# Fused attention, MLP and expert layer on one core: another order in the attention step, the experts' choice behind the loop, one product for two bounds

## The chip, the core and the metric

The kernel runs on one core of a Trainium2 chip. TensorE (PE) multiplies, VectorE (DVE), ScalarE (ACT) and GpSimd (POOL) do the elementwise work, SyncE (SP) issues most of the DMAs, GpSimd the indirect ones. Each engine works through its own instructions in the order of the program and waits for the others at semaphores. The metric is the time of one execution on the device in microseconds (us).

## The reference

Three layers, one behind the other, in float32. The attention's rows keep their 32 largest scores only; the last layer sends each of 2304 tokens to one of eight experts.

```python
def _attn_ref(q, k, v):                       # 4 batches, 8 heads, 576 rows, 64 wide
    scores = np.matmul(q, k.transpose(0, 1, 3, 2)) / np.sqrt(64)
    kth = np.partition(scores, -32, axis=-1)[..., -32:-31]
    scores = np.where(scores >= kth, scores, -1e9)
    attn = np.exp(scores - scores.max(-1, keepdims=True))
    attn = attn / (attn.sum(-1, keepdims=True) + 1e-9)
    return np.matmul(attn, v)

def _moe_ref(x, w_in, w_out):                 # x [2304, 512], w_in [512, 2048]
    h = x @ w_in
    return (h * np.clip(h + 3.0, 0.0, 6.0) / 6.0) @ w_out

def _moe2_ref(x, expert_emb, tau, w1, w2):    # 8 experts, 512 -> 1024 -> 512
    logits = normalised(x) @ normalised(expert_emb).T / tau
    expert_idx = np.argmax(logits, axis=1)
    gate_w = softmax(logits)[np.arange(N), expert_idx]
    for e in range(8):
        mask = expert_idx == e
        out[mask] = gate_w[mask, None] * (np.maximum(x[mask] @ w1[e], 0.0) @ w2[e])
```

## The kernel before

**Loop.** `step` (L776) runs 76 times. The attention is cut into 72 units of 128 rows and two heads each ("t" units, and "r" units that collect the last 64 rows of each batch and score twice as much). A unit passes through five steps: in step i unit i is scored (`scores`, `take`, `pairs`), unit i-1 selects (`select`, `bounds`), i-2 is masked (`relu`, `mask`), i-3 exponentiated and scaled (`expo`, `guard`, `inverse`, `scale`), i-4 transposed and multiplied with V (`turned`, `keep`, `values`, `finish`). The order of the calls in `step` is the order of instructions on each engine; nothing rearranges it inside the loop. "A step" below is one round of it.

**Selection.** `pairs` (L373) splits a row's 576 scores on VectorE into maxima and minima, so that `select` (L386) finds the 32 largest in four rounds of MAX8 (eight at a time) with MATCH_REPLACE8 between them. Round 3 then multiplies the 32nd value by 2^100 (`zb`, L405), the bias of the `relu` (L416) that makes the mask. `bounds` (L407) makes -max/8 (`nb`, L410) on GpSimd, the bias of the exponential (L426).

**Banks.** `turned` (L446) makes nine transposes a unit, three per PSUM bank, in two banks (`bank_t`) by turns, so that the third group writes the bank of the first; `keep` (L455) copies them out on ScalarE. The routing below uses the same two banks.

**MLP beside it.** Finished rows come in pairs of 128-token groups; each pair gives eight items of the MLP queue (`push_group`, L514), one taken per step, save in eight steps (`PAUSE`, L39). An item is `s1` (24 products, L530), `gate`, `swish` (L540), `large`, `small` (`gl`, L547, on GpSimd), and one step later `s2` (12 products, L563) in two halves. The MLP's weights are read in pieces and split into high and low parts in `words` and `split_w` in the first 23 steps or so.

**Routing.** Each finished group of 128 tokens pushes four pieces on the queue `side` (`route`, L580), one taken at the end of each step: `r1` transposes, `r2` the logits and the argmax (L606 to L609), `r4` the place of each token within its expert by two small products with `tri` and `ones` (L615, L616) and a running sum `acc` on GpSimd, `r5` the place's number (L626, L627) and an indirect scatter of the token's number to the table `tbl` (L628).

**Behind the loop** the MLP's remaining items run (`whole`, two `side` pieces before each), and there the framework's scheduler sets the order by its own priorities. Once 16 groups are placed, `order` (L663) sorts the experts by load; their weights are loaded, tokens gathered from `tbl` (`tokens`, L744), and the experts run (`stage1` L906, `stage2` L922).

## Time and profile before

| | us |
|---|---|
| median of 3 runs (lowest, highest) | 1187.98 (1187.89, 1189.08) |
| the profiled execution | 1184.85 |
| its span, first to last instruction | 1183.1 |
| busy: PE, DVE, ACT, POOL | 1026.0, 838.1, 732.1, 645.7 |

The span divides into the loop (to about 770 us), the rest of the MLP (to about 892 us) and the experts. Busy times are to be read by stretch: VectorE has two thirds of its work in the loop, TensorE is busy nearly throughout. TensorE's granted clock changes between 1.2 and 2.4 GHz; a clock of 0.76 in a window means that it was at the lower level for about half of it.

### The profile page before, as it was taken

To read this page: it belongs to the slowest core of one execution; us is meant where nothing else is said; L and a number is where in the kernel's file an instruction comes from. 1 tells how busy PE (TensorE), PEld (TensorE's weight loads), DVE (VectorE), ACT (ScalarE), POOL (GpSimd) and SP (SyncE) were. 2 spreads that over 40 slices of the span, in tenths; PEclk is the share of its full clock that TensorE was granted. 3 is DMA by queue.
4 is the path that set the end of the run, shared out by engine and by line. 5 is a ranking of instruction groups with operands and counts; after the bars stand their busy time and mean duration, and the time that the engine had idled before them with its cause. 6 is when DMAs were issued, how large, how long until landed. Compare 5 with 4: busy or idle time off the path is not lost. (4 is left out here: it accounts for less than half of the span.)

```text
span 1183.1 us, 21477 instructions
## 1 busy us (share of the span) xinstructions
PE 1026.0 (87%) x7224; PEld 885.8 (75%) x7224; DVE 838.1 (71%) x2714; ACT 732.1 (62%) x1518; POOL 645.7 (55%) x846
## 2 busy tenths in 40 slices
PE   2476766699999899999899999999998898999994
PEld 1354555578888788888788878889987787888883
DVE  6999977998899998899998899611244343445440
ACT  5688768777777877777877787642334343444540
POOL 5667767686777786777786766623231433113200
PEclk9966778789999999999999998999998899999997
DMA  7335555655324445424454333346781564244540
GB/s 212 120 100 174 164 177 187 195 179 197 122 90 155 127 160 184 121 89 155 115 183 157 121 92 115 110 142 178 210 276 32 187 217 171 71 176 147 174 166 20
DMA packets 97113, 176.49 MB, mean 149 GB/s; under 512 B 21135, under 2 KB 46882, under 8 KB 96991
## 3 DMA queue, kind: packets, MB, share of 16 engines
q1 hardware_dynamic: 92351, 164.90, 43.4%
q0 software_dynamic: 4640, 10.10, 2.5%
q8 instruction: 60, 0.98, 0.3%
q14 instruction: 62, 0.51, 0.1%
HBM read 155.87 MB, written 19.71 MB: 148 GB/s over the span
## 5 line engine op out<-in xcount | busy, mean ns | idle before, releaser
L420 POOL TENSOR_TENSOR s<-s,z 128x576 f32<-128x576 f32 x144 | 186.0, 1292 | 13.0 <-ACT z L416 11.5
L530 PE MATMUL bank_h<-xh,vh 128*128 128x256 f32 x576 | 172.1, 299 | 2.7 <-ACT xh L488 1.6
L530 PE MATMUL bank_h<-xh,lo 128*128 128x256 f32 x576 | 166.7, 289 | 7.1 <-DMA lo<-lo_dram 7.1
L530 PE MATMUL bank_h<-xl,vh 128*128 128x256 f32 x576 | 166.2, 288 | 0.6 <-DVE xl L489 0.6
L399 DVE MAX8 A<-left 128x8 f32<-128x288 f32 (+1 forms) x288 | 160.0, 596 | 0.0
L453 PE MATMUL bank_t<-ident,s 128*128 128x128 f32 x648 | 110.2, 297 | 53.1 <-ACT s L440 26.1
L547 POOL TENSOR_TENSOR gl<-u,gh 128x512 fp32r<-128x512 f32 x72 | 93.2, 1294 | 79.0 <-ACT gh L544 78.0
L453 PEld LDWEIGHTS bank_t<-ident,s 128*128 128x128 f32 x648 | 76.1, 149 | 75.8 <-ACT pt L458 37.7
L368 PE MATMUL ps_sc<-kst,qh 128*128 128x288 f32 x256 | 88.8, 359 | 49.1 <-ACT s L371 24.1
L536 ACT ACTIVATE u<-bank_h,half 128x512 f32<-128x512 f32 x72 | 49.5, 687 | 118.9 <-PE bank_h L530 118.9
L563 PE MATMUL y<-wh,gh 128*128 128x512 f32 x288 | 120.0, 418 | 0.0
L530 PEld LDWEIGHTS bank_h<-xh,vh 128*128 128x128 f32 x576 | 113.3, 197 | 8.1 <-issue 3.1
L530 PEld LDWEIGHTS bank_h<-xh,lo 128*128 128x128 f32 x576 | 113.2, 196 | 8.3 <-DMA lo<-lo_dram 8.3
L563 PE MATMUL y<-lo,gh 128*128 128x512 f32 x288 | 115.9, 403 | 0.0
L530 PEld LDWEIGHTS bank_h<-xl,vh 128*128 128x128 f32 x576 | 113.4, 197 | 1.4 <-DVE xl L489 1.0
L735 DVE TENSOR_TENSOR l<-a,h 128x1024 fp32r<-128x1024 f32 x64 | 77.4, 1232 | 51.9 <-ACT h L734 45.7
L563 PE MATMUL y<-wh,gl 128*128 128x512 f32 x288 | 114.2, 401 | 0.0
L416 ACT ACTIVATE z<-s,zb 128x576 bf16<-128x576 f32 x144 | 112.7, 782 | 1.0 <-DVE zb L405 0.8
L426 ACT ACTIVATE s<-s,nb 128x576 f32<-128x576 f32 x144 | 111.7, 775 | 0.0
L458 ACT COPY pt<-bank_t 128x384 f32<-128x384 f32 x216 | 95.6, 479 | 24.4 <-PE bank_t L453 24.4
L540 DVE SCALAR_TENSOR_TENSOR u<-u,bank_h 128x512 f32<-128x512 f32 x72 | 49.2, 684 | 83.8 <-ACT u L536 83.7
L471 PE MATMUL bank_a<-pt,vt 128*64 128x128 f32 (+1 forms) x1600 | 105.4, 285 | 0.0
(230 smaller groups left out, 2819.9 us busy)
## 6 DMA issues: line engine op xcount, KB each, us to landing
lo<-lo_dram SPq DMA_DIRECT2D x144, 512.0 KB, 4.3
a<-in_moe_w_dram SPq DMA_DIRECT2D x64, 512.0 KB, 8.7
kraw<-in_k_dram SPq DMA_DIRECT2D x64, 144.0 KB, 2.6
qraw<-in_q_dram SPq DMA_DIRECT2D x64, 128.0 KB, 3.3
w<-in_moe_w_in_dram SPq DMA_DIRECT2D x32, 256.0 KB, 3.9
w<-in_moe_w_out_dram SPq DMA_DIRECT2D x32, 256.0 KB, 3.5
lo_dram<-wf SPq DMA_DIRECT2D x32, 256.0 KB, 2.1
vt<-in_v_dram SPq DMA_DIRECT2D x16, 320.0 KB, 4.1
```

Source lines behind the costliest of these rows:

```text
L368: nc.tensor.matmul(ps[:, n, :HS], t, kk[:, HS * g:HS * g + HS], start=(o == 0), stop=(o == len(parts) - 1))
L399: nc.vector.max(A[:, n, 8 * r:8 * r + 8], src[:, n, :w])
L416: nc.scalar.activation(zb_[n], tile_of(i, n), AF.Relu, bias=sel[i][2][:, n:n + 1], scale=-BIG)
L420: nc.gpsimd.tensor_tensor(s, s, zb_[n], op=ALU.subtract)
L426: nc.scalar.activation(s, s, AF.Exp, bias=sel[i][1][:, n:n + 1], scale=SCALE, accum_out=sums[i][:, n:n + 1])
L453: nc.tensor.transpose(pp[:, 128 * k:128 * k + 128], e[:, 128 * (3 * c + k):128 * (3 * c + k) + 128], ident)
L458: nc.scalar.copy(pts[i][:, 3 * c:3 * c + 3, :].rearrange("p k n -> p (k n)"), tb_.pop((i, c))[:, :384])
L471: nc.tensor.matmul(av[64 * n:64 * n + 64, c0:c1], vt[:, k, 64 * n:64 * n + 64], pt[:, k + 5 * n if k < 4 else 4, c0:c1], start=(o == 0), s ...
L530: nc.tensor.matmul(ph[:, a, :], w, x[:, k, :], start=(k == 0 and n == 0), stop=(k == 3 and n == 2))
L547: nc.gpsimd.tensor_tensor(state[q][1], state.pop((q, "u")).rearrange("p (a n) -> p a n", a=2), state[q][0].bitcast(F32), op=ALU.subtract)
L563: nc.tensor.matmul(state["y"][o], x[:, a, c], w, start=(f == 0 and n == 0), stop=(f == 15 and n == 2))
L735: nc.vector.tensor_tensor(lo, x, hi.bitcast(F32), op=ALU.subtract)
```

## The change

1. **Another order of `step`.** `mask` of head 0 moves behind `select` round 0; rounds 0 and 1 no longer stand together; `relu`, `expo`, `select` and `take` are interleaved with the three `turned`/`keep` pairs, and a half of `s2` (`after`) now stands between the first and the second use of the banks, the other half behind the third. `inverse` (the reciprocal of the sums) stands before `select` round 3 instead of behind it. The `side` piece (`aside`) is taken in mid-step.
2. **One product for both bounds.** `bounds` makes `-max/8` and `2^100 * 32nd` in one GpSimd product of two operands (128x4); the two `zb` products on VectorE go. It stands behind `scale`, ahead of `mask` of head 1, and the first `relu` of the next step now waits for it.
3. **The experts' choice in batches.** `r2` ends with the copy of the logits; `r4` and `r5` go. `choose` does the argmax, the places and the scatters for all groups scored since the last call, behind the loop, for 12, 2, 2 and 2 groups. The scatters are declared independent of each other.

```diff
@@ -400,20 +406,17 @@
         if r < TOPK // 8 - 1:
             for n in range(2):
                 nc.vector.match_replace(dst[:, n, :w], A[:, n, 8 * r:8 * r + 8], src[:, n, :w], NEG)
-        else:
-            for n in range(2):
-                nc.vector.tensor_scalar(zb[:, n:n + 1], A[:, n, TOPK - 1:TOPK], BIG, None, op0=ALU.mult)
 
     def bounds(i):
 
-        A, nb, zb = sel[i]
-        nc.gpsimd.tensor_scalar(nb, A[:, :, 0], -SCALE, None, op0=ALU.mult)
+        A, nb = sel[i]
+        nc.gpsimd.tensor_tensor(nb, A[:, :, 0:TOPK:TOPK - 1], kb, op=ALU.mult)
         if not exact:
             nc.gpsimd.tensor_tensor(viol[:, i, :, :], A[:, :, TOPK - 1:TOPK].broadcast_to([128, 2, 2]), A[:, :, 15:24:8], op=ALU.subtract)
 
     def relu(i, n):
 
-        nc.scalar.activation(zb_[n], tile_of(i, n), AF.Relu, bias=sel[i][2][:, n:n + 1], scale=-BIG)
+        nc.scalar.activation(zb_[n], tile_of(i, n), AF.Relu, bias=sel[i][1][:, n, 1:2], scale=-BIG)
 
     def mask(i, n):
         s = tile_of(i, n)
...
@@ -423,7 +426,7 @@
         if n == 0:
             sums[i] = sm.tile([128, 2], F32, tag="sums", name="sums")
         s = tile_of(i, n)
-        nc.scalar.activation(s, s, AF.Exp, bias=sel[i][1][:, n:n + 1], scale=SCALE, accum_out=sums[i][:, n:n + 1])
+        nc.scalar.activation(s, s, AF.Exp, bias=sel[i][1][:, n, 0:1], scale=SCALE, accum_out=sums[i][:, n:n + 1])
 
     def guard(i):
         sel.pop(i)
...
@@ -599,39 +602,47 @@
...
             nc.vector.tensor_copy(l_all[:, g, :], p2)
-            ix = sm.tile([128, 8], U32, tag="ix", name="ix")
-            ixf = sm.tile([128, 1], F32, tag="ixf", name="ixf")
-            oh = sm.tile([128, E], BF16, tag="oh", name="oh")
-            mx = sm.tile([128, 8], F32, tag="mx", name="mx")
-            nc.vector.max(mx, l_all[:, g, :])
-            nc.vector.max_index(ix, mx, l_all[:, g, :])
-            nc.vector.tensor_copy(ixf, ix[:, 0:1])
-            nc.vector.tensor_scalar(oh, iota8, ixf, None, op0=ALU.is_equal)
-            state["oh"] = oh
-
-        def r4():
-            oh = state["oh"]
-            pq = bank()[:, :E]
-            nc.tensor.matmul(pq, tri, oh, start=True, stop=False)
-            nc.tensor.matmul(pq, ones, acc, start=False, stop=True)
-            nc.gpsimd.tensor_tensor(acc, acc, oh, op=ALU.add)
-            po = sm.tile([128, E], F32, tag="po", name="po")
-            nc.vector.tensor_tensor(po, pq, ebase, op=ALU.add)
-            state["po"] = po
-
-        def r5():
-            oh, po = state["oh"], state["po"]
-            de = sm.tile([128, 1], F32, tag="de", name="de")
-            di = sm.tile([128, 1], I32, tag="di", name="di")
-            nc.vector.scalar_tensor_tensor(po, po, 1.0, oh, op0=ALU.mult, op1=ALU.mult, accum_out=de)
-            nc.vector.tensor_copy(di, de)
-            nc.gpsimd.indirect_dma_start(out=tbl, out_offset=bass.IndirectOffsetOnAxis(ap=di[:, 0:1], axis=0),
-                                         in_=ids[:, g, :], in_offset=None)
-            done_groups[0] += 1
-            if done_groups[0] == NG - 2:
-                order()
-
-        side.extend((r1, r2, r4, r5))
+            scored[0] += 1
+
+        side.extend((r1, r2))
+
+    def choose():
+
+        g0, g1 = done_groups[0], scored[0]
+        n = g1 - g0
+        lg = l_all[:, g0:g1, :]
+
+        def wide(x):
+            return x.unsqueeze(2).broadcast_to([128, n, E])
+
+        def deep(x):
+            return x.unsqueeze(1).broadcast_to([128, n, E])
+        nc.vector.tensor_reduce(mxs[:, g0:g1], lg, axis=AX.X, op=ALU.max)
+        eq = fs.tile([128, NG, E], F32, tag="df", name="eqs")[:, :n, :]
+        nc.vector.tensor_tensor(eq, lg, wide(mxs[:, g0:g1]), op=ALU.is_equal)
+        nc.vector.tensor_tensor(eq, eq, deep(rev8), op=ALU.mult)
+        first = fs.tile([128, NG], F32, tag="gt", name="first")[:, :n]
+        nc.vector.tensor_reduce(first, eq, axis=AX.X, op=ALU.max)
+        nc.vector.tensor_tensor(picks[:, g0:g1, :], eq, wide(first), op=ALU.is_equal)
+        for g in range(g0, g1):
+            nc.gpsimd.tensor_tensor(before[:, g + 1, :], before[:, g, :], picks[:, g, :], op=ALU.add)
+        pq = half_a()[:, :n * E]
+        nc.tensor.matmul(pq, tri, picks[:, g0:g1, :].rearrange("p g e -> p (g e)"), start=True, stop=False)
+        nc.tensor.matmul(pq, ones, before[:, g0:g1, :].rearrange("p g e -> p (g e)"), start=False, stop=True)
+        po = fs.tile([128, NG, E], F32, tag="df", name="pos")[:, :n, :]
+        nc.vector.tensor_tensor(po, pq.rearrange("p (g e) -> p g e", e=E), deep(ebase), op=ALU.add)
+        nc.vector.tensor_tensor(po, po, picks[:, g0:g1, :], op=ALU.mult)
+        de = fs.tile([128, NG], F32, tag="nrm", name="de")[:, :n]
+        nc.vector.tensor_reduce(de, po, axis=AX.X, op=ALU.add)
+        nc.vector.tensor_copy(rows[:, g0:g1], de)
+        for g in range(g0, g1):
+            w_ = nc.gpsimd.indirect_dma_start(out=tbl, out_offset=bass.IndirectOffsetOnAxis(ap=rows[:, g:g + 1], axis=0),
+                                              in_=ids[:, g, :], in_offset=None)
+            tc.declare_no_dep(w_.ins, group="places", reason="every token has one place")
+            tc.add_to_no_dep_group("places", w_.ins)
+        done_groups[0] = g1
+        if g1 == NG - 2:
+            order()
 
     def whole(item, last):
 
...
@@ -785,44 +796,50 @@
                 convert_w()
 
         a = moe.popleft() if moe and i not in PAUSE else None
+        def aside():
+            if side:
+                side.popleft()()
+
+        def after(o):
+            if last:
+                last[6](last[0], o)
+
         at_(2, relu, 0)
-        at_(2, mask, 0)
         at_(3, expo, 0)
-        lows()
         split_w()
         load_k(i + 2)
         at_(1, select, 0)
-        at_(1, select, 1)
         part(a, 1)
         part(a, 2)
+        at_(2, mask, 0)
+        lows()
+        at_(4, turned, 0)
+        at_(4, keep, 0)
         part(a, 3)
         words()
-        for c in range(2):
-            at_(4, turned, c)
-            at_(4, keep, c)
+        aside()
+        part(a, 4)
+        after(0)
+        at_(4, turned, 1)
+        at_(4, keep, 1)
         at_(0, scores, 0)
         at_(4, turned, 2)
+        at_(3, expo, 1)
+        at_(1, select, 1)
+        at_(0, take, 0)
         at_(4, keep, 2)
-        at_(0, take, 0)
+        after(1)
         at_(1, select, 2)
+        part(a, 5)
+        at_(3, guard)
         words()
-        at_(3, expo, 1)
-        at_(3, guard)
-        if last:
-            last[6](last[0], 0)
-        part(a, 4)
-        part(a, 5)
         at_(0, scores, 1)
         at_(0, take, 1)
-        at_(1, select, 3)
         at_(3, inverse)
         if i - 3 >= EARLY:
             at_(3, scale)
+        at_(1, select, 3)
         at_(2, relu, 1)
-        at_(2, mask, 1)
-        at_(1, bounds)
-        if last:
-            last[6](last[0], 1)
         split_w()
         at_(0, pairs)
         words()
...
@@ -835,9 +852,9 @@
             at_(3, scale)
         at_(4, values)
         at_(4, finish)
+        at_(1, bounds)
+        at_(2, mask, 1)
         need_v(i)
-        if side:
-            side.popleft()()
         if i in (12, 14, 15, 17):
             embed((12, 14, 15, 17).index(i))
         if i == 20:
...
@@ -876,6 +895,9 @@
                 if side:
                     with tc.high_priority(offset=SIDE):
                         side.popleft()()
+                if done_groups[0] < scored[0] and scored[0] % 2 == 0:
+                    with tc.high_priority(offset=SIDE):
+                        choose()
             last = whole(moe.popleft() if moe else None, last)
             if rest and len(moe) <= 1:
                 rest = False
```

`kb` is a constant tile with -1/8 and 2^100, `rev8` one with 8 to 1, `before` holds the running sums in place of `acc`.

**VectorE, one step in mid-loop**, from the last operation of the value products (`xl`) to the next `pairs` (MAX and MATCH_REPLACE are the rounds of `select`, L540/L543 is `swish`, `sums` the reciprocal). Before:

```order
L489 TENSOR_TENSOR xl<-bank_a,xh 128x128
L399 MAX A<-top 128x8 x2
L402 MATCH_REPLACE top<-A,top 128x144 x2
L399 MAX A<-top 128x8 x2
L402 MATCH_REPLACE left<-A,top 128x144 x2
L540 SCALAR_TENSOR_TENSOR u<-u,bank_h 128x512
L399 MAX A<-left 128x8 x2
L402 MATCH_REPLACE left<-A,left 128x288 x2
L399 MAX A<-left 128x8 x2
L405 TENSOR_SCALAR zb<-A 128x1 x2
L433 RECIPROCAL sums<-sums 128x2
L380 TENSOR_TENSOR ps_sc<-ps_sc,s_144 128x2x144
```

Now:

```order
L492 TENSOR_TENSOR xl<-bank_a,xh 128x128
L405 MAX A<-top 128x8 x2
L408 MATCH_REPLACE top<-A,top 128x144 x2
L543 SCALAR_TENSOR_TENSOR u<-u,bank_h 128x512
L405 MAX A<-top 128x8 x2
L408 MATCH_REPLACE left<-A,top 128x144 x2
L405 MAX A<-left 128x8 x2
L408 MATCH_REPLACE left<-A,left 128x288 x2
L436 RECIPROCAL sums<-sums 128x2
L405 MAX A<-left 128x8 x2
L386 TENSOR_TENSOR ps_sc<-ps_sc,s_149 128x2x144
```

The two `zb` rows are gone, `swish` stands behind round 0 instead of round 1, and the reciprocal ahead of the last MAX.

**TensorE, the same place in a step**: `bank_t` are the transposes, `ps_sc` the scores, `y` the second MLP product. Before:

```order
L453 MATMUL bank_t_120<-ident,s_145 128x128 x3
L453 MATMUL bank_t_121<-ident,s_145 128x128 x3
L368 MATMUL ps_sc<-kst,qh 128x288
L368 MATMUL ps_sc<-kst,ql 128x288
L368 MATMUL ps_sc<-kst,qh 128x288
L368 MATMUL ps_sc<-kst,ql 128x288
L453 MATMUL bank_t_120<-ident,s_145 128x128 x3
L563 MATMUL y<-wh,gh 128x512
L563 MATMUL y<-lo_6130,gh 128x512
```

Now:

```order
L566 MATMUL y<-wh,gh 128x512
L566 MATMUL y<-lo_5897,gh 128x512
L566 MATMUL y<-wh,gl 128x512
L566 MATMUL y<-wh,gh 128x512
L566 MATMUL y<-lo_5897,gh 128x512
L566 MATMUL y<-wh,gl 128x512
L456 MATMUL bank_t_125<-ident,s_150 128x128 x3
L374 MATMUL ps_sc<-kst,qh 128x288
L374 MATMUL ps_sc<-kst,ql 128x288
L374 MATMUL ps_sc<-kst,qh 128x288
L374 MATMUL ps_sc<-kst,ql 128x288
L456 MATMUL bank_t_126<-ident,s_150 128x128 x3
```

Six products of `s2` stand between the first three transposes (the row ahead of these) and the second three; the scores, and the third three, follow.

**GpSimd behind the loop**: `tbl` are the scatters, `gl` the low part that `s2` waits for. Before:

```order
L547 TENSOR_TENSOR gl<-u,gh 128x512
L442 TENSOR_SCALAR s_146<-s_146,sums 128x576 x2
L547 TENSOR_TENSOR gl<-u,gh 128x512 x2
L617 TENSOR_TENSOR acc<-acc,oh 128x8
L628 DMA tbl<-ids,di 22528x2
L547 TENSOR_TENSOR gl<-u,gh 128x512
L617 TENSOR_TENSOR acc<-acc,oh 128x8
L628 DMA tbl<-ids,di 22528x2
L547 TENSOR_TENSOR gl<-u,gh 128x512 x8
```

Now:

```order
L550 TENSOR_TENSOR gl<-u,gh 128x512
L433 TENSOR_SCALAR sums<-sums 128x2
L445 TENSOR_SCALAR s_151<-s_151,sums 128x576 x2
L550 TENSOR_TENSOR gl<-u,gh 128x512
L639 DMA tbl<-ids,rows 22528x2 x12
L550 TENSOR_TENSOR gl<-u,gh 128x512 x2
L628 TENSOR_TENSOR before<-before,picks 128x8 x2
L550 TENSOR_TENSOR gl<-u,gh 128x512 x2
L639 DMA tbl<-ids,rows 22528x2 x2
L550 TENSOR_TENSOR gl<-u,gh 128x512 x7
```

Where a scatter stood alone between two `gl`, twelve now stand in a row ahead of one.

## Rows read from the trace of the kernel before

**Rows 1.** Windows of the whole run: us; busy us (count) per engine; PE clock; DMA share; GB/s
```profile
15.00:135.00 120.00, 70.91 (x365) 54.89 (x365) 117.26 (x409) 89.91 (x196) 81.75 (x107) 0.76 0.47 147
135.00:270.00 135.00, 97.91 (x686) 83.09 (x687) 116.76 (x379) 97.73 (x214) 97.74 (x129) 0.82 0.57 184
270.00:740.00 470.00, 450.11 (x3653) 390.77 (x3653) 433.55 (x1568) 360.18 (x795) 337.41 (x468) 0.99 0.42 134
740.00:900.00 160.00, 154.77 (x1097) 138.40 (x1094) 49.70 (x160) 65.88 (x128) 53.58 (x61) 1.00 0.56 175
```

**Rows 2.** Windows again: one plain step (first row), then stretches of thinner or fuller steps
```profile
335.00:344.40 9.40, 9.40 (x78) 8.17 (x77) 8.42 (x32) 6.98 (x16) 6.73 (x11) 1.00 0.38 129
353.70:371.70 18.00, 16.02 (x151) 13.76 (x150) 15.93 (x60) 13.37 (x32) 11.31 (x16) 1.00 0.57 183
390.50:431.80 41.30, 35.48 (x291) 30.46 (x290) 39.81 (x135) 32.91 (x78) 32.40 (x44) 0.96 0.47 148
528.50:546.60 18.10, 16.12 (x151) 13.80 (x150) 15.96 (x60) 13.45 (x32) 11.36 (x16) 1.00 0.57 185
565.30:605.50 40.20, 34.06 (x293) 29.04 (x292) 39.55 (x134) 32.93 (x78) 31.65 (x43) 1.00 0.50 155
694.50:708.90 14.40, 11.77 (x111) 8.85 (x110) 14.30 (x56) 12.68 (x30) 11.83 (x17) 1.00 0.28 88
```

**Rows 3.** Lines of VectorE by form: operations the change removes; busy us, mean ns
```profile
L405 DVE TENSOR_SCALAR zb<-A 128x1 f32<-128x1 f32 x144 | 19.4, 144 | 0.0
...
L626 DVE SCALAR_TENSOR_TENSOR po<-po,oh 128x8 f32<-128x8 f32 x18 | 11.4, 631 | 0.2
...
L609 DVE TENSOR_SCALAR oh<-iota,ixf 128x8 bf16<-128x8 f32 x18 | 9.3, 519 | 0.6
...
L606 DVE MAX8 mx<-l_all 128x8 f32<-128x8 f32 x18 | 3.1, 170 | 0.6
...
L607 DVE FIND_INDEX8 ix<-mx,l_all 128x8 uint32<-128x8 f32 x18 | 2.9, 160 | 0.0
L619 DVE TENSOR_TENSOR po<-bank_t,ebase 128x8 f32<-128x8 f32 x18 | 2.8, 157 | 5.6 <-PE bank_t L616 5.6
L608 DVE CAST ixf<-ix 128x1 f32<-128x1 uint32 x18 | 2.8, 153 | 0.6
L627 DVE CAST di<-de 128x1 int32<-128x1 f32 x18 | 2.7, 153 | 0.5
```

**Rows 4.** One line of VectorE, all its instructions: ns min/median/max
```profile
L626 DVE SCALAR_TENSOR_TENSOR po<-po,oh x18: 157/647/1147, 307.0 to 909.7; 128x8 f32<-128x8 f32 x18
```

**Rows 5.** Lines of GpSimd by form: the present product and the two-operand one beside it
```profile
L410 POOL TENSOR_SCALAR nb<-A 128x2 f32<-128x2 f32 x72 | 17.3, 240 | 0.0
...
L412 POOL TENSOR_TENSOR viol<-A 128x4 bf16<-128x4 f32 x72 | 15.7, 219 | 2.6 <-DVE zb L405 2.4
```

**Rows 6.** Timeline of TensorE in the plain step: start, us; third transposes of the step
```profile
340.30 0.29 PE L368 MATMUL ps_sc<-kst,ql 128*128 128x288 f32 x1
340.56 0.55 PE L453 MATMUL bank_t<-ident,s 128*128 128x128 f32 x3
```

**Rows 7.** Timelines of VectorE, ScalarE and GpSimd, same step: what the reciprocal's place decides
```profile
342.35 1.41 DVE L399 MAX8 A<-left 128x8 f32<-128x576 f32 x2
...
342.05 0.79 ACT L426 ACTIVATE s<-s,nb 128x576 f32<-128x576 f32 x1
...
343.02 0.22 POOL L430 TENSOR_SCALAR sums<-sums 128x2 f32<-128x2 f32 x1 [2.33 <-ACT s L426]
```

**Rows 8.** Timeline of GpSimd behind the loop: rhythm of gl, two indirect transfers in a row
```profile
818.49 1.29 POOL L547 TENSOR_TENSOR gl<-u,gh 128x512 fp32r<-128x512 f32 x1 [4.33 <-ACT gh L544]
...
869.90 0.99 POOL L750 DMA_INDIRECT xg<-y_dram,idt  x1 [2.03 <-DMA idt<-tbl]
871.19 0.96 POOL L750 DMA_INDIRECT xg<-y_dram,idt  x1 [0.30 <-issue]
```

**Rows 9.** Timeline of TensorE, last group's routing: its wait ahead of the product with tri
```profile
909.14 0.17 PE L615 MATMUL bank_t<-oh,tri 128*128 128x8 bf16 x1 [4.37 <-DVE oh L609]
```

More of the change, by code (lines that the diff above doesn't have):

```diff
@@ L509, in layers @@
     step = [0]
-    done_groups = [0]
+    done_groups, scored = [0], [0]
     pushed = [0]
@@ L665, in order @@
         pc = half_a()
-        nc.tensor.matmul(pc[:, :E], ones, acc, start=True, stop=True)
+        nc.tensor.matmul(pc[:, :E], ones, before[:, NG - 2, :], start=True, stop=True)
         cnt = fs.tile([1, E], F32, tag="cnt", name="cnt")
@@ L687, in finish_counts @@
         pc = half_a()
-        nc.tensor.matmul(pc[:, :E], ones, acc, start=True, stop=True)
+        nc.tensor.matmul(pc[:, :E], ones, before[:, NG, :], start=True, stop=True)
         cnt = fs.tile([1, E], F32, tag="cnt2", name="cnt2")
```

18 lines of the change are left out of this document (12 added, 6 removed).

## The prediction

> **What bounds the kernel now.** I read the windows of the whole run first, to see which engine fills which stretch, then the same view for single steps, then VectorE's lines for the price of what goes, and timelines for the places where the order changes.
>
> The windows [rows 1] show three regimes. From 15 to 135 us VectorE is busy 117.26 of 120 us: this stretch is its own. From 135 to 270 us it is busy 116.76 of 135, TensorE's granted clock is 0.82 (part of the time at 1.2 GHz), and waits for weight pieces lie between. From 270 to 740 us TensorE is busy 450.11 of 470 and VectorE 433.55, so the mean does not say which one decides. From 740 to 900 us TensorE has 154.77 of 160, VectorE and GpSimd a third each.
>
> The 470 us come apart in the single steps [rows 2]. The plain step, with a whole MLP item, has TensorE busy 9.40 of 9.40 us and VectorE 8.42: TensorE's. The five stretches below it hold the steps whose MLP item was paused and those that load new keys. There VectorE is busy 15.93 + 39.81 + 15.96 + 39.55 + 14.30 = 125.6 of 132 us, TensorE 113.5: VectorE's. In what is left of the 470 us, 338 us, TensorE is busy 450.1 - 113.5 = 336.7. So VectorE's time is worth something in 132 us of the main loop and next to nothing in the other 338.
>
> **The change, part by part.**
>
> *The two zb products* cost 19.4 us in 144 instructions [rows 3], 0.27 us a step. In the first stretch of VectorE, about 12 steps, that is 12 x 0.27 = 3.2 us. In the second, about 10 steps at a busy share of 116.76/135, it is 10 x 0.27 x 0.87 = 2.3 us. In the five stretches, 14 steps, it is 3.8 us. In the plain steps it is nothing: the cover is TensorE's 9.40 us, and VectorE would merely wait longer for the MLP's rows.
>
> *The argmax and the places* leave the loop: the other seven rows of the group add up to 35.0 us for 18 groups, 1.94 a group [rows 3]; the logits' copy stays. Twelve groups are routed between 270 and 740 us, 23.3 us; in proportion to time, 132/470 of it, 6.5 us, lies in steps that VectorE bounds. Of this 11.4 us is one operation on 8 columns whose single instructions took from 157 to 1147 ns [rows 4], so most of it was waiting. The Trainium skill has a rule for this (SBUF — State Buffer, "SBUF: two separate sides"): VectorE and GpSimd share a pair of ports under an exclusive lock, and an operation with two SBUF inputs waits while GpSimd holds it. By that rule the wait would pass to the next such operation, the whole group would be worth no more than seven times the unblocked 157 ns, 1.1 us instead of 1.94, and the sum would lose 2.8 us. I keep the 6.5, because the selection's MAX and MATCH rows, which follow in the loop, have one input.
>
> So VectorE's stretches of the main loop give 3.8 + 6.5 = 10.3 us. From below nothing excludes 0, if another engine's chain is just behind; from above TensorE's 113.5 of 132 us allow 18.
>
> *What is put in their place.* `choose` runs where VectorE is busy 49.70 of 160 us [rows 1]; its nine operations on up to 96 columns, four times, are covered there, and I cost them at nothing (without that cover 36 operations at about 0.16 us, 6 us). The product for both bounds replaces one GpSimd instruction of 240 ns by one of a kind that takes 219 ns beside it [rows 5]: nothing.
>
> *The banks.* In the plain step the third three transposes start 0.26 us after the last score product, which took its place in the pipeline in about 0.13 us [rows 6]: the rest, 0.13 us, is the wait for the copy that frees the first bank. With six products of `s2` between the two uses this wait goes; but TensorE then changes its kind of work once more per step, and the same rows show such a change costing about as much. Bounds over some 35 plain steps: 0 and -4.5 us. I take -1.5.
>
> *The new waits.* The first `relu` of a step waits for GpSimd's product where it waited for VectorE's. ScalarE is busy 6.98 of 9.40 us in a plain step [rows 2], which covers a fraction of a microsecond; queued behind that `relu` are the exponential and the MLP's `gate`, and VectorE's `swish` waits for these. The reciprocal, now ahead of the last MAX, makes VectorE wait for `guard`; see the rivals.
>
> *Scatters.* Eighteen in the loop and behind it become 12 + 2 + 2 + 2. They did not wait for each other before, being a step or more apart, so the declared independence gives nothing by itself. Two indirect transfers in a row start 1.29 us apart [rows 8], so twelve hold GpSimd for 15.5 us. Behind the loop it makes one `gl` per MLP item, 1.29 us, and idles 4.33 between [rows 8]. One `gl` is then late by 15.5 - 4.3 = 11.2 us, and `s2` waits for it. The scheduler has drawn the first MLP products of the next three items ahead of that `s2`; at half of the 5.62 us of an item each, that is 8.4 us of work. What stays is 2.8 us of idle TensorE; bounds 0 and 11.2.
>
> *The end.* The last group's product with `tri` waits 4.37 us on TensorE before [rows 9]. Now 50 products of the expert layer stand between its logits and `tri`, and 24 fewer ahead of the logits. At 5.62/36 = 0.16 us each, the 26 more are 4.1 us, which fills the wait; the chain to the gathered tokens is as long as it was, plus one scatter of 1.29 us, because both of the last pair's stand behind it. I take +1.3, between 0 and 5.
>
> **Sum.** -3.2 - 2.3 - 10.3 - 1.5 + 2.8 + 1.3 = -13.2 us. Against the profiled execution's 1184.85 that is 1171.7; the median of the runs is 3.1 higher, so 1174.8, rounded to 1175.
>
> **Rivals.**
>
> *The reciprocal becomes VectorE's new wait (slower).* In the plain step the last MAX starts at 342.35, the exponential that `guard` needs at 342.05, and `guard` itself at 343.02 and for 0.22 [rows 7]. A reciprocal asked for at 342.35 would have waited 0.9 us. For it: the slack is negative by the old timing. Against it: on ScalarE the `take` of the first half and the third copy stood ahead of that exponential and now stand behind, which brings it forward by about as much. The price at 0.9 us in the 12 + 10 + 14 steps that VectorE bounds is 32 us: 1207. It decides from 0.4 us a step on, where it eats the 13.2 and 2.4 more. Chance 0.10.
>
> *The saving is hidden.* If in the five stretches and at the start ScalarE's or GpSimd's chain stands close behind VectorE (in 390.5 to 431.8 us they are busy 32.91 and 32.40 of 41.30 [rows 2]), the 15.8 us shrink to some 5, and the 4.1 added behind the loop cancel them: 1187. For it speaks that each step is one long chain through four engines, against it that VectorE's share is 95%. Chance 0.12.
>
> *The scatters are not covered.* If the reordered MLP products run out or wait for their one bank, the whole 11.2 us fall on TensorE, and the wait at the end grows by 5: +8.4 + 3.7, 1187. Chance 0.07, counted half to no change and half to slower.
>
> *TensorE's clock comes up earlier.* In 135 to 270 us it was at the lower level for about 2 x 0.18 of the time, 49 us [rows 1]. The main loop, where TensorE is busy 450.11 of 470 us, shows 0.99. If work between the banks' uses closes some, the stretch shrinks towards VectorE's 116.76 - 2.7 = 114 us: at most 21 us, at two thirds 14. That gives 1161. The Trainium skill says the same of the cause (TensorE: Matmul & The Clock Gate, "What's actually happening"): the throttled clock is the default, and activity releases it. Against it: VectorE and the weight pieces set the pace there, and they change little. Chance 0.13.
>
> That the change does not do what it says I give no chance: the order of the instructions shows each part.
>
> **Numbers.** Forecast 0.58, at 1175; with the two unknown costs and the cover at their ends it spans 1160 to 1185. A measurement of this kernel can tell about 0.2%, 2.4 us, from no change. Faster: 0.58 + 0.13 = 0.71. Same: 0.12 + 0.04 = 0.16. Slower: 0.10 + 0.03 = 0.13. The range takes in the clock's case and the hidden one up to a little more: 1154 to 1192; outside are most of the reciprocal's case and the deep end of the clock's.
>
> **What would show it.** Right: the plain step still at 9.3 to 9.4 us with TensorE busy throughout; the five stretches shorter by a half to one microsecond a step; the stretch from 15 us on shorter by 0.27 us a step; one idle stretch of TensorE of some 3 us right behind the loop, while GpSimd issues twelve scatters. Wrong: a line of waits of the reciprocal on `guard` of more than 15 us in total; waits of `relu` on the new product; plain steps that change by more than 0.3 us either way; a granted clock in 135 to 270 us that differs by more than 0.05.

## The result: 1.0% slower on the record, and no gain in any series

| | before | changed |
|---|---|---|
| median of 4 runs, us | 1188.49 (1187.89 to 1189.08) | 1200.16 (1196.88 to 1205.69) |
| ratio, 95% interval | | 1.0103 [1.0059, 1.0147] |
| profiled execution, its span, us | 1184.85, 1183.1 | 1196.88, 1195.1 |
| forecast, us | | 1175, range 1154 to 1192 |

The changed kernel was run twice more, beside the kernel before each time (after_again, after_third below): 1.0099 [1.0067, 1.0131] and 1.0017 [0.9994, 1.0041]. In the first two of its three profiles TensorE's signals behind the loop came late; the third, which has none, is the one to read behind the loop (last section). None of the three shows the 1.1% that were forecast as a gain.

First the windows of the changed kernel, the columns as in [rows 1]:

```profile
15.00:135.00 120.00, 70.39 (x365) 55.41 (x365) 117.44 (x380) 90.05 (x195) 80.82 (x107) 0.74 0.47 147
135.00:270.00 135.00, 97.06 (x687) 81.92 (x686) 117.73 (x360) 98.55 (x214) 103.69 (x131) 0.82 0.57 186
270.00:740.00 470.00, 442.43 (x3618) 392.80 (x3617) 404.42 (x1369) 359.24 (x791) 320.99 (x444) 0.99 0.42 134
740.00:900.00 160.00, 145.38 (x1004) 129.86 (x1003) 53.21 (x137) 62.62 (x117) 65.47 (x83) 0.97 0.56 172
```

From 15 to 135 us VectorE runs 29 instructions fewer than before and is busy as long (117.44 against 117.26). From 270 to 740 us it is busy 29.1 us less, but the steps have not become shorter (next table): TensorE is busy 7.7 us less, too. The clock in the second stretch is the same 0.82. From 740 to 900 us TensorE is busy 9.4 us less.

The starts of two products, `values` (a step's last work on TensorE) and `s2` (an MLP item's), mark the stages; steps, units and items are counted from 0, and step i holds the `values` of unit i-4. Differences to the profile of before, us; the first row holds the starts in before:

| | `values` of step 10 | step 20 | step 75, the loop's last | `s2` of item 60 | end |
|---|---|---|---|---|---|
| before | 111.1 | 256.2 | 786.3 | 821.6 | 1183.1 |
| changed, on record | +0.1 | -1.3 | +0.3 | +9.3 | +12.0 |
| changed, third profile | +0.2 | +0.3 | +4.6 | +6.8 | +3.9 |
| forecast | -3.2 | -5.5 | -17.3 | -14.5 | -13.2 |

The loop misses its forecast by 17.6 us on record and by 21.9 in the third profile. Behind the loop 4.1 us more were forecast; on record it is 11.7, in the third profile 0.7 less than before. So the first question is where the 17 us went that the loop was to lose; late signals (last section) stand in the stretch of the other.

### The profile page after: what moved, and what is told of

Its sections match the earlier page's. It is cut to its first block, busy times and chain, and to the rows that moved or that the text cites. A ratio compares the mean times of both kernels' runs of the same rounds, so it can differ in the third digit from the quotient of the medians.

```text
span 1195.1 us, 21149 instructions
## 1 busy us (share of the span) xinstructions
PE 1022.0 (86%) x7196; PEld 891.6 (75%) x7196; DVE 815.8 (68%) x2443; ACT 735.5 (62%) x1518; POOL 646.3 (54%) x849
## 5 line engine op out<-in xcount | busy, mean ns | idle before, releaser
L423 POOL TENSOR_TENSOR s<-s,z 128x576 f32<-128x576 f32 x144 | 183.5, 1291 | 32.1 <-ACT z L419 30.5
L374 PE MATMUL ps_sc<-kst,qh 128*128 128x288 f32 x256 | 93.5, 376 | 69.5 <-ACT s L377 40.0
L456 PE MATMUL bank_t<-ident,s 128*128 128x128 f32 x648 | 114.7, 292 | 41.4 <-ACT s L443 27.6
L456 PEld LDWEIGHTS bank_t<-ident,s 128*128 128x128 f32 x648 | 83.2, 149 | 59.0 <-ACT s L443 33.1
L543 DVE SCALAR_TENSOR_TENSOR u<-u,bank_h 128x512 f32<-128x512 f32 x72 | 49.5, 688 | 113.8 <-ACT u L539 108.4
L377 ACT COPY s<-ps_sc 128x576 f32<-128x576 f32 x144 | 91.6, 636 | 54.0 <-PE ps_sc L374 53.0
L566 PE MATMUL y<-wh,gh 128*128 128x512 f32 x288 | 123.8, 431 | 0.0
L374 PEld LDWEIGHTS ps_sc<-kst,qh 128*128 128x128 f32 x256 | 55.8, 218 | 89.9 <-ACT s L377 42.2
L419 ACT ACTIVATE z<-s,nb 128x576 bf16<-128x576 f32 x144 | 112.1, 779 | 8.1 <-POOL nb L413 7.8
```

The costliest lines, as they stand in the source:

```text
L374: nc.tensor.matmul(ps[:, n, :HS], t, kk[:, HS * g:HS * g + HS], start=(o == 0), stop=(o == len(parts) - 1))
L377: nc.scalar.copy(sbuf[i % NS][:, :, HS * g:HS * g + HS], ps_[i][:, :, :HS])
L419: nc.scalar.activation(zb_[n], tile_of(i, n), AF.Relu, bias=sel[i][1][:, n, 1:2], scale=-BIG)
L423: nc.gpsimd.tensor_tensor(s, s, zb_[n], op=ALU.subtract)
L456: nc.tensor.transpose(pp[:, 128 * k:128 * k + 128], e[:, 128 * (3 * c + k):128 * (3 * c + k) + 128], ident)
L543: nc.vector.scalar_tensor_tensor(u, u, 1.0, state.pop((q, "h")), op0=ALU.min, op1=ALU.mult)
```

## The experiments

Theory: VectorE's saving is real, but each step is one chain through four engines, and the new order puts other work of GpSimd beside VectorE's. Rivals: one part of the change costs by itself (the choice, the bounds, the reciprocal's wait), or the scatters do.

**The three parts, each alone, on the kernel before.** The product for both bounds alone (e1):

```diff
-        nc.gpsimd.tensor_scalar(nb, A[:, :, 0], -SCALE, None, op0=ALU.mult)
+        nc.gpsimd.tensor_tensor(nb, A[:, :, 0:TOPK:TOPK - 1], kb, op=ALU.mult)
...
-        nc.scalar.activation(zb_[n], tile_of(i, n), AF.Relu, bias=sel[i][2][:, n:n + 1], scale=-BIG)
+        nc.scalar.activation(zb_[n], tile_of(i, n), AF.Relu, bias=sel[i][1][:, n, 1:2], scale=-BIG)
```

> The kernel before, with the one GpSimd product for both bounds in place of the two zb products, and nothing else. Theory 'the saving turns into port waits': VectorE loses 19.4 us of instructions, but its operations with two SBUF inputs (the kst and wf subtractions, the selection of the place) get longer, as they did in the changed kernel (kst 767 to 1006 ns, wf 502 to 583 ns); about 3 us are left: 1185 us. Rival 'the saving is real, the order eats it': 5.5 us at the start and 3.8 in the paused steps come through, 1179 us, and kst and wf keep their means within 5%. Rival 'hidden': 1188 us with VectorE idle longer.

Measured: 1210.43, 1.0176 [1.0125, 1.0228], outside all three; the loop ends 26.8 us later than before, while `kst` and `wf` keep their means (793 and 511 ns). Waits of ScalarE, 135 to 740 us (waiter <- awaited: us in total, times, longest), in this kernel:

```profile
ACT z L414 <- POOL nb L408: 67.2, 43, 4.4
```

and in the changed kernel:

```profile
ACT z L419 <- POOL nb L413: 3.3, 7, 1.7
```

In the old order `nb` stands on GpSimd behind `mask 1`, and `relu` waits for it 43 times. The new order moves `bounds` ahead of that mask; without it the part costs 1.8%.

The choice alone (e2):

```diff
-        side.extend((r1, r2, r4, r5))
+            scored[0] += 1
+        side.extend((r1, r2))
+    def choose():
```

> The kernel before, with the choice of experts batched behind the loop (12, 2, 2, 2 groups) and nothing else. Theory 'the batch stalls TensorE behind the loop': the loop ends some 5 us earlier (786 to about 781), and the twelve scatters in a row then delay one gl by 11 us, so that everything from the product with that gl on is 6 us later than before, and the end is 1194 to 1198 us. Rival 'the new order is what costs': the stall behind the loop is under 4 us here, and the time is 1180 to 1184 us.

Measured: 1187.75, 1.0006 [0.9979, 1.0033], between the two. VectorE is busy 413.00 us from 270 to 740 us instead of 433.55, and the loop ends 1.8 us earlier (3.5 and 4.5 in the profiles of e10 and e16, whose loop is the same). Most of the rest has become waits. VectorE's waits from 135 to 740 us, before:

```profile
DVE u L540 <- ACT u L536: 30.1, 26, 5.5
DVE ps_sc L380 <- ACT s L371: 6.1, 11, 1.0
...
DVE sums L433 <- POOL sums L430: 2.6, 3, 1.1
```

and with the choice taken out:

```profile
DVE u L545 <- ACT u L541: 51.9, 37, 5.0
```

`swish` waits 21.8 us more for ScalarE's `gate`: about what was saved. `gate` itself waits for TensorE's `s1`, from 270 to 740 us here

```profile
ACT u L541 <- PE bank_h L535: 67.1, 40, 4.9
```

and 66.9 us before. Only 4.8 of the 21.8 us lie in the five stretches that the prediction gave to VectorE; most of the others lie in steps where it expected this wait. Behind the loop the batch costs 9.6 us up to `s2` of item 57 and 6.7 up to item 60.

The order alone (all the moves in `step` that the diff shows, with the two `zb` products and the choice left where they were; e3):

```diff
         at_(2, relu, 0)
-        at_(2, mask, 0)
         at_(3, expo, 0)
-        lows()
...
         part(a, 2)
+        at_(2, mask, 0)
+        lows()
+        at_(4, turned, 0)
+        at_(4, keep, 0)
```

> The kernel before, with the new order of the step and nothing else (two zb products, choice in the loop). Theory 'the new order adds waits': with the second round of the selection behind swish, VectorE waits for ScalarE's gate some 18 us more, 9 us more for take and 10 us more for guard than before; plain steps are 0.2 us shorter, steps in which xl or a key is late are 1 us longer; together 1190 to 1196 us. Rival 'the order is a gain': plain steps 0.2 us shorter and nothing else, 1181 us (35 x 0.2 us).

Measured: 1198.20, 1.0087 [1.0058, 1.0116]; the loop ends 16.4 us later. The reciprocal's wait came as said (14.8 us instead of 2.6), that for `gate` by half (38.9 instead of 30.1), that for `take` did not. Then order and bounds without the choice, which stays in the loop (e4):

```diff
-        side.extend((r1, r2))
+        side.extend((r1, r2, r4, r5))
```

> The changed kernel with the choice of experts put back into the loop, one group at a time (the bounds' product and the new order stay). Theory 'the batch stalls TensorE behind the loop': without twelve scatters in a row the 11 us behind the loop are gone, the routing's 27 us of VectorE are back in the loop and cost some 5 to 8 of them: 1190 to 1196 us. Rival 'the batch is free': 1200 us or more, because the routing is back and nothing is won behind the loop.

Measured: 1193.36, 1.0057 [1.0037, 1.0077], as its theory had it; the loop +12.6 us. The parts don't add: +26.8, -1.8 and +16.4 alone, +0.3 to +4.6 together (+3.3 in the second profile). In the new order the choice does cost about 8 to 12 us in the loop, in the old one 1.8 to 4.5.

What the order does on VectorE is seen in its lines by form, 15 to 740 us (busy us, mean ns), first before, then the changed kernel:

```profile
L221 DVE SCALAR_TENSOR_TENSOR wf<-w 128x256 int32<-128x256 int32 x62 | 29.0, 502 | 4.1 <-DMA w<-in_moe_w_in_dram 3.4 <-DMA w<-in_moe_w_out_dram 0.7
...
L352 DVE TENSOR_TENSOR kst<-kraw,kst 64x288 fp32r<-64x288 f32 x28 | 20.4, 767 | 0.4
```

```profile
L227 DVE SCALAR_TENSOR_TENSOR wf<-w 128x256 int32<-128x256 int32 x62 | 33.9, 583 | 1.5 <-DMA w<-in_moe_w_out_dram 1.2 <-DMA w<-in_moe_w_in_dram 0.2
L358 DVE TENSOR_TENSOR kst<-kraw,kst 64x288 fp32r<-64x288 f32 x28 | 27.1, 1006 | 0.4
```

The same two operations, the same in form and number, take 11.6 us more: over half of the 18.9 us of `zb` in this window. (`kst`, the keys' remainder, is a part of `lows` and was moved with it.) The order alone has them at 551 and 939 ns, the choice alone at 512 and 737. And the operation on 8 columns of [rows 4] does get shorter in the new order, while another one gets longer. Before:

```profile
L626 DVE SCALAR_TENSOR_TENSOR po<-po,oh 128x8 f32<-128x8 f32 x11 | 10.2, 927 | 0.0
L609 DVE TENSOR_SCALAR oh<-iota,ixf 128x8 bf16<-128x8 f32 x11 | 7.3, 665 | 0.4
```

and with the order alone:

```profile
L609 DVE TENSOR_SCALAR oh<-iota,ixf 128x8 bf16<-128x8 f32 x11 | 14.3, 1303 | 0.4
L626 DVE SCALAR_TENSOR_TENSOR po<-po,oh 128x8 f32<-128x8 f32 x10 | 2.5, 251 | 0.0
```

The sum, 17.5 and 16.8 us, stays nearly the same, as if a wait had only changed its place.

**Single moves of the order taken back, in the changed kernel.** The forecasts of this part start from the record's 1200 us, which holds the late signals of the last section; the profiles of e5, e6, e7 and e9 have none. So the loop's end is compared, and not the time: 786.6, 789.6 and 790.9 us in the three profiles of the changed kernel. Its VectorE waits, 135 to 740 us:

```profile
DVE u L543 <- ACT u L539: 48.5, 41, 6.6
DVE ps_sc L386 <- ACT s L377: 13.3, 22, 1.5
DVE sums L436 <- POOL sums L433: 12.4, 20, 1.5
```

The second selection back beside the first (e5):

```diff
         at_(1, select, 0)
+        at_(1, select, 1)
...
-        at_(1, select, 1)
```

> The changed kernel (1200 us) with the selection's second round back beside the first, ahead of s1. Theory 'VectorE idles for gate': the second round, 1.1 us of VectorE work, again covers its wait for ScalarE's gate; the wait of swish, 48.5 us between 135 and 740 us, falls to some 30, the loop (786.6 us) gets 5 to 8 us shorter, the time is 1192 to 1195 us. Rival 'that wait is only slack of steps that TensorE bounds': the loop stays within 2 us, 1199 to 1201 us.

The reciprocal back behind the last selection (e6):

```diff
+        at_(1, select, 3)
         at_(3, inverse)
         if i - 3 >= EARLY:
             at_(3, scale)
-        at_(1, select, 3)
```

> The changed kernel with reciprocal and scale back behind the last MAX. Theory 'the reciprocal waits for guard on VectorE': its 12.4 us of waits between 135 and 740 us go, those in steps that VectorE bounds count: 3 to 6 us less, 1194 to 1197 us. Rival 'the early reciprocal helps': scale and the first transposes come 1.4 us later per step and the time grows by 3 us or more, to 1203 us.

Mask 0 and the low parts back at the head of the step (e7):

```diff
         at_(2, relu, 0)
+        at_(2, mask, 0)
         at_(3, expo, 0)
+        lows()
...
-        at_(2, mask, 0)
-        lows()
```

> The changed kernel with GpSimd's first mask of a step and the lows (the remainders of keys and queries) back ahead of the selection. Theory 'the moved mask lies beside the keys' remainder on VectorE and holds it up': kst falls from 1006 to some 770 ns and wf from 583 to 510 ns, 11 us of VectorE, of which 3 to 6 come through in the steps that load keys: 1194 to 1197 us. Rival 'the waits only change their place': another operation with two SBUF inputs gets longer by as much, 1199 to 1201 us.

Measured: 1191.82, 1.0048 [1.0023, 1.0073]; 1195.04, 1.0075 [1.0056, 1.0094]; 1183.82, 0.9980 [0.9957, 1.0003]. The loop ends 7.7 and 8.0 us later than before, and 1.2 us earlier. The first two theories fall, though the times are at the numbers forecast or next to them: the loop got longer than the changed kernel's. In e5 the wait moves from `u` to the reciprocal,

```profile
DVE sums L436 <- POOL sums L433: 53.8, 46, 3.6
DVE u L543 <- ACT u L539: 15.4, 12, 6.0
```

and in e6 from VectorE to GpSimd, whose scaling now waits for the later reciprocal (19.5 us in the changed kernel):

```profile
POOL s L445 <- DVE sums L436: 67.8, 50, 2.4
```

In e5 there is one thing more: `wf` takes 490 ns in the first stretch (15 to 135 us) instead of 608, and step 10 comes 3.1 us earlier than before, which is what the prediction gave that stretch. No other kernel has that; it is one profile.

The third theory holds for `kst`, which takes 638 ns there, less than before the change, and not for `wf` (570 ns; 619 in the first stretch). The kernels with this repair end the loop at 785.1, 783.7 and 782.2 us (e7, e11, e14). The low parts alone moved back (e12):

```diff
         at_(3, expo, 0)
+        lows()
...
-        lows()
```

> The changed kernel with the lows alone back ahead of the selection; the first mask stays where the change put it. Theory 'the key remainders, not the mask, are what was moved to the wrong place': as e7, 0.2% under before or better, kst near 640 ns on VectorE. Rival 'the mask': as the changed kernel, kst near 1000 ns.

1185.69, 0.9989 [0.9971, 1.0007]; `kst` 851 ns, between the two, so both moves lengthen it. From e12 to e7 only GpSimd's mask stands elsewhere, and `kst` on VectorE takes 213 ns less. The loop's end, +1.9 us, lies within those of the changed kernel.

The routing piece at the step's end, where it was, on order and bounds with the choice in the loop (e8, made from e4):

```diff
         words()
-        aside()
...
         need_v(i)
+        aside()
```

> The changed kernel with the choice in the loop (1193 us), and the routing pieces back at the end of the step. Theory 'pieces in the middle of the step are what made the choice dear under the new order': the loop's end falls from 12.6 us behind the kernel before to under 4 us behind, 1183 to 1187 us. Rival 'it is the rest of the order': it stays within 3 us, 1190 to 1195 us.

1198.41, 1.0078 [1.0048, 1.0109], later than both forecasts and with late signals; the loop +11.4 us against +12.6 without the move: the piece's place is not the cause.

**The twelve scatters.** In the third profile of the changed kernel GpSimd, right behind the loop:

```profile
795.90 1.22 POOL L639 DMA_INDIRECT tbl<-ids,rows  x1 [7.12 <-DVE rows L637]
797.43 0.97 POOL L639 DMA_INDIRECT tbl<-ids,rows  x1 [0.30 <-issue]
...
810.08 0.96 POOL L639 DMA_INDIRECT tbl<-ids,rows  x1 [0.30 <-issue]
811.06 2.53 POOL L550 TENSOR_TENSOR gl<-u,gh 128x512 fp32r<-128x512 f32 x2
```

Twelve in 15.2 us (15.5 by [rows 8]), and two `gl` wait for the last. They were then pulled apart, one pair behind each of the next six MLP items; each pair's rows are formed with 0 times that item's rounded hidden values added, which ties them to it (e9):

```diff
-        nc.vector.tensor_copy(rows[:, g0:g1], de)
-        for g in range(g0, g1):
+        spots.extend(range(g0, g1, 2))
...
             last = whole(moe.popleft() if moe else None, last)
+            if spots and last:
+                scatter(recent[0])
```

> The changed kernel with the twelve scatters of the first batch made to follow one another in pairs, each pair behind the gl of another MLP item (its rows are formed from the item's gh, times zero, by two small VectorE operations a pair); the choice itself stays batched. Theory 'the twelve scatters in a row stall TensorE behind the loop': the 6.0 us of idle TensorE at 804 us go, everything from there on is 6 to 11 us earlier, 1189 to 1194 us. Rival 'the items behind the loop wait for their own chain': the idle stretch stays above 4 us and the time is 1198 to 1201 us.

1190.18, 1.0029 [1.0001, 1.0058]: the time came true, but beside the changed kernel without late signals (1.0017) it is no gain. From the loop's end to `s2` of item 57 this kernel loses nothing (+2.5 to +1.7 us), the third profile of the changed one 5.1 (+4.6 to +9.7). The same in the old order with the choice batched (the edits of e2 and e9; e10):

> The kernel before with the batched choice alone (1188 us), and its first twelve scatters in pairs behind the gl of six items. Theory 'the scatters in a row are what the batch costs': the 9 us by which it fell behind at the item after the loop go, 1179 to 1183 us. Rival 'they come back in the items that now carry scatters': 1186 to 1189 us.

1191.79, 1.0008 [0.9988, 1.0027], with late signals, and the same kernel in another series (e16):

> The kernel of e10 (old order of the step, batched choice, spread scatters) in another series. Theory 'the new order with the bounds' product is worth little even when repaired': 1180 to 1184 us, within 3 us of e14's 1181. Rival 'the repaired order carries the gain': 1186 us or more, as before.

1185.95, 0.9987 [0.9967, 1.0008], at the rival's edge. From the loop's end to item 60 these two lose 0.9 and 0.4 us, where e2 lost 6.7. But it comes back: from item 60 to the end the third profile of the changed kernel and e2 gain 2.9 and 2.8 us on before, e9 and e16, with the scatters apart, lose 3.6 and 3.0 (e14 and e15 below 1.0 and 0.3). So the stall is real and the repair removes it there; that it shortens the whole is not shown.

**Together, and the kernel again.** The edits of e7 and e9 in the changed kernel, in two series (e11, e14), and the changed kernel in each (after_again, after_third). The late signals named there are shown in the last section:

> The changed kernel itself, beside the variants on the same chip. Its first profile has idle stretches of ScalarE and VectorE behind the loop that nothing in the profile ends (8.0 us before a gate, 5.0 before a swish, 27.4 before the expert layer's remainders); three variants whose code is the same there lack them and run that part 9 to 13 us faster. Theory 'they belong to that execution, not to the change': 1187 to 1193 us here. Rival 'they belong to this program': 1197 to 1203 us again, with the same stretches at the same places.

> The changed kernel with both repairs: first mask and lows early, and the scatters spread. Theory 'the two costs lie in different places and add': 1184 us less the 6 us that e7 still lost between the items at the loop's end, 1177 to 1180 us. Rival 'the spread scatters only delay later items, as the 4 us did that the first spread kernel lost at 838 us': 1183 to 1187 us.

> The changed kernel once more. Both profiles of it so far, and all four of the last series (one chip), have 14 to 19 products of TensorE behind the loop whose signal the waiting engines see 1 to 9 us late; the eight profiles of the two other series have none. Theory 'that is the chip or the execution, and half of what the changed kernel lost is not its own': beside a series without late signals it is slower than before by 0.2 to 0.6% only, 1189 to 1194 us against 1186.5. Rival 'the changed kernel brings it about, or the loss is elsewhere': slower by 0.9 to 1.2% again, 1197 to 1201 us against 1186.5.

> The kernel of e11 (early mask and lows, scatters spread) in another series. Theory 'its two repairs add where the tail is undisturbed': 1177 to 1181 us against 1186.5, 3 us or more under e12. Rival 'the spread scatters only move the wait': within 2 us of e12.

Changed: 1202.16, 1.0099 [1.0067, 1.0131], and 1189.34, 1.0017 [0.9994, 1.0041]. With both edits: 1187.88, 0.9979 [0.9949, 1.001], and 1181.07, 0.9956 [0.9936, 0.9977], without late signals. after_again came out by its rival, after_third and e14 by their theories, e11 by neither. The lines of the two conversions in e14:

```profile
L228 DVE SCALAR_TENSOR_TENSOR wf<-w 128x256 int32<-128x256 int32 x62 | 32.9, 567 | 2.8 <-DMA w<-in_moe_w_out_dram 1.4 <-DMA w<-in_moe_w_in_dram 1.4
...
L359 DVE TENSOR_TENSOR kst<-kraw,kst 64x288 fp32r<-64x288 f32 x28 | 17.3, 655 | 0.4
```

One stall of the new order was left. In the changed kernel TensorE stands still inside `s1` when two new groups begin:

```profile
346.04 0.28 PE L533 MATMUL bank_h<-xh,vh 128*128 128x256 f32 x1
347.02 0.39 PE L533 MATMUL bank_h<-xl,vh 128*128 128x256 f32 x1 [0.70 <-DVE xl L492]
```

because `xl` stands on VectorE behind five operations of `pairs`, the last of them

```profile
345.95 0.45 DVE L389 TENSOR_TENSOR top<-ps_sc,left 128x288 f32<-128x288 f32 x1
346.31 0.45 DVE L390 TENSOR_TENSOR left<-ps_sc,left 128x288 f32<-128x288 f32 x1
346.68 0.28 DVE L492 TENSOR_TENSOR xl<-bank_a,xh 128x128 fp32r<-128x128 f32 x1
```

so in the steps that end groups `xl` was put ahead of these last two, on top of the edits of e7 and e9 (e15):

```diff
-        at_(0, pairs)
+        at_(0, pairs, 0 if ends else None)
...
         at_(4, finish)
+        if ends:
+            at_(0, pairs, 1)
```

> The kernel of e14 (early mask and lows, spread scatters) in which, in the steps that finish a pair of groups, the remainder xl stands ahead of the last two operations of pairs on VectorE. Theory 'the new order puts VectorE 1.2 us later in the step, so that s1 of a new pair of groups waits 0.98 us for xl': those stalls (8 of them, with what comes behind them 1.0 to 1.2 us each) go, 1172 to 1176 us where e14 had 1181. Rival 'the stall is covered elsewhere': within 2 us of e14.

1179.19, 0.9922 [0.9897, 0.9947]: the lowest time, its median 8.2 us below that of its before (1187.41), but not the 1172 to 1176 of the theory. In that kernel `xl` comes in time:

```profile
443.29 0.28 DVE L495 TENSOR_TENSOR xl<-bank_a,xh 128x128 fp32r<-128x128 f32 x1
443.49 0.45 DVE L392 TENSOR_TENSOR top<-ps_sc,left 128x288 f32<-128x288 f32 x1
```

```profile
443.62 0.39 PE L536 MATMUL bank_h<-xl,vh 128*128 128x256 f32 x1
```

and TensorE's 2.8 us of waits on `xl` from 270 to 740 us (four, not eight) are gone; the ten steps 38 to 47 take 96.2 us instead of 97.7. That the whole gets shorter by it is not shown: the loops of e14 and e15 end at 782.2 and 782.3 us, and the intervals of the two, from different series, overlap.

## Why the prediction was wrong

The step that failed is the one from VectorE's busy time to the length of a stretch. It took two things for granted: that instructions removed there leave the others as long as they were, and that time removed on the busiest engine is time gained.

- **"So VectorE's stretches of the main loop give 3.8 + 6.5 = 10.3 us": failed.** From step 20 to the loop's end, the banks included, +1.6 (on record) and +4.3 (third profile) were measured instead of -11.8. The five stretches of [rows 2] tell both halves. Their sums, taken between the same `values`: before, the choice alone (e2), the changed kernel on record, and mask and low parts back in it (e7):

```profile
sum 132.00, PE 113.45 PEld 95.91 DVE 125.55 ACT 105.34 POOL 98.55; mean PE 22.69 PEld 19.18 DVE 25.11 ACT 21.07 POOL 19.71
sum 129.70, PE 111.97 PEld 94.94 DVE 118.73 ACT 102.98 POOL 99.48; mean PE 22.39 PEld 18.99 DVE 23.75 ACT 20.60 POOL 19.90
sum 133.90, PE 110.52 PEld 95.86 DVE 122.81 ACT 104.97 POOL 96.99; mean PE 22.10 PEld 19.17 DVE 24.56 ACT 20.99 POOL 19.40
sum 132.70, PE 111.68 PEld 97.51 DVE 115.38 ACT 104.85 POOL 95.18; mean PE 22.34 PEld 19.50 DVE 23.07 ACT 20.97 POOL 19.04
```

In the changed kernel VectorE's work there fell by 2.7 us only, since the remaining operations got longer. In e7 it fell by 10.2, as forecast, and the stretches are 0.7 us longer than before (with the same moves 0.8 and 0.9 longer in e11 and e15, 2.0 shorter in e14). With the choice alone it fell by 6.8, and 2.3 came through (some 3.6 in e10 and e16).

- **What the saved time became** is seen in the first of the five. Waits in the changed kernel from 354.0 to 364.3 us:

```profile
PE y L566 <- DMA lo<-lo_dram: 2.2, 1, 2.2
ACT pt L461 <- PE bank_t L456: 1.6, 1, 1.6
POOL sums L433 <- ACT s L429: 3.2, 1, 3.2
DVE sums L436 <- POOL sums L433: 1.5, 1, 1.5
```

The half of `s2` that the change moved ahead waits for a low part (of the MLP's weights) that a DMA still brings; behind it the transposes, `keep`, the exponential, `guard` and VectorE's reciprocal follow, each a wait of the next engine. Before, neither TensorE's nor VectorE's wait stood there; in the third profile they are 3.2 and 3.7 us. From below the prediction had said that nothing excludes 0 "if another engine's chain is just behind", and that is what came.
- **"In the first stretch of VectorE ... 3.2 us", "in the second ... 2.3 us": failed**, measured -0.5 to +0.2 at step 10 and -1.4 to +0.1 from there to step 20 in three profiles. The `zb` instructions went, but in the first stretch `wf<-w` grew from 15.2 to 18.2 us for its 32 instructions. Moving mask and low parts back does not help there (e7); with the selection's second round beside the first again `wf` is short and the 3.1 us are there (e5). The prediction priced what VectorE issues and gave no term to what the new order puts beside it. No run joins e5's move with e7's.
- The rule on VectorE's and GpSimd's ports (the Trainium skill, SBUF — State Buffer, "SBUF: two separate sides") was set aside for the 6.5 us. The traces agree with it in that `po` and `kst`, which have two SBUF inputs, change their length with the order (`po` 927 to 251 ns in e3; `kst` 851 to 638 from e12 to e7, where GpSimd's mask alone moves); that a lock is the cause no run here shows, and `oh`, with one wide input, changes as well. The prediction's corollary, that the wait passes to the next such operation, fits e3 and not e7, where VectorE's work gets less.
- **The banks, -1.5:** right in sign. A plain step went from 9.32 to 9.12 us, 0.2 a step where 0.13 was the most that was worked out; no run shows that the banks alone did it. It was given back: a step that begins two groups now takes 10.36 us (9.63 in e15, with `xl` early), and the ten steps 38 to 47 take 97.7 us, 96.7 before.
- **The reciprocal as VectorE's new wait:** the wait came, 12.4 us against 2.6 (14.8 in the third profile), near the 15 named as the mark. It is not the cause: taking it away (e6) was slower than leaving it.
- **`relu` on the new product:** rightly small, 3.3 us, but only because the order moves with it (e1).
- **The scatters, +2.8:** about right. +2.2 from the loop's end to item 60 in the third profile, where TensorE waits 3.5 us for `gl`; +9.0 on record, where late signals lie in the same stretch. At item 57 it is 5.1, of which 2.9 is caught up.
- **The end, +1.3:** -2.9 in the third profile, +2.7 on record. The wait ahead of `tri` [rows 9] is gone, as worked out; but TensorE's wait for the gathered tokens grew from 4.5 to 9.2 us.
- **The clock rival:** 0.82 before and after; it did not come up.

The rival "the saving is hidden" (1187) had the right mechanism in one half, the chain behind VectorE, and with 1.0017 its time too; the other half, that operations get longer, stands in no rival, and by the sum only as the 2.8 us that the prediction set aside. That 1189.34, the third series, would lie in the range is no merit: the forecast gain is not there either. On record there are some 12 us more behind the loop than in the third profile.

In one series e15 stands at 0.9922 [0.9897, 0.9947] and e16, the old order with the same choice and scatters, at 0.9987 [0.9967, 1.0008] of the same before: the mended kernel, new order and bounds' product together, is the faster one. But its gain is not in the loop. That ends at 782.2 and 782.3 us in the profiles of e14 and e15, at 782.8 and 781.8 in those of e10 and e16, which have the choice taken out but the old order. The two differ behind it, 396.3 us to the end in e15 and 400.2 in e16; why is open.

## What to carry to other kernels

Where a step is one chain through four engines, an instruction saved on the busiest is worth what the next engine in the chain leaves over: read which wait follows it before adding up durations (10.2 us less work on VectorE in five stretches of e7, and none of it gained). When work is moved, price also the operations of the neighbour engine that will now run beside it, since their durations are not constants (`kst`: 638 to 1010 ns by order alone). Work batched behind a loop holds its engine in one piece (twelve scatters, 15.2 us); spread, it no longer stalls there, but look whether the time comes back later.

## What was not expected of the hardware

In some profiles a consumer starts microseconds after the product it waits for. On record, TensorE behind the loop:

```profile
798.33 0.95 PE L603 MATMUL bank_t<-ent,yt 128*128 128x8 f32 x8
...
803.02 0.28 PE L533 MATMUL bank_h<-xh,lo 128*128 128x256 f32 x1
...
810.26 0.58 PE L533 MATMUL bank_h<-xh,vh 128*128 128x256 f32 x1 [5.83 <-DVE u L543]
```

its consumer on VectorE, and that of the `s1` product on ScalarE:

```profile
803.00 0.17 DVE L604 COPY l_all<-bank_t 128x8 f32<-128x8 f32 x1 [2.88 <-remote]
```

```profile
808.80 0.69 ACT L539 ACTIVATE u<-bank_h,half 128x512 f32<-128x512 f32 x1 [7.97 <-remote]
```

The products ended at 799.3 and 803.3 us; their readers start 3.7 and 5.5 us later, and TensorE, which needs what they make, stands for 5.83. In the third profile of the same kernel the same product and copy lie next to each other:

```profile
802.69 0.95 PE L603 MATMUL bank_t<-ent,yt 128*128 128x8 f32 x8
```

```profile
803.68 0.17 DVE L604 COPY l_all<-bank_t 128x8 f32<-128x8 f32 x1 [0.31 <-PE bank_t L603]
```

Signals of TensorE seen over 1 us after their product: 19 on record, 14 to 19 in the profiles of after_again, e8, e10 and e11, none in the other profiles, after_third, e14 and e16 (the kernels of after_again, e11 and e10) among them. So it is not the program's alone, nor the chip's: after_again and after_third ran on the same one. From the loop's end to the end of the program the record's profile is 11.7 us longer than before, the third's 0.7 shorter; the late signals stand in that stretch, but that they make all of the difference is not shown. Their cause is open.
